# A gated linear attention with a MoE-style MLP behind it: every queue ordered by a list-scheduling model, loads reordered, dummy matmuls first, groups of 2 chunks

## The chip, the cores and the metric

One core of a Trainium2 chip. The metric is the device time of one execution in microseconds (us). A ratio is the mean time of one kernel's fast runs over that of the other's fast runs of the same rounds, so it is not quite the ratio of the medians that are quoted. A span is the profiled execution's time; it is mostly 1.6 to 2 us less than the time of the run. Rounds are the turns in which kernels were measured together.

## The reference

```python
# attention: batch 4, 8 heads, 768 steps, head_dim 48
for t in range(S):
    state = alpha[:, :, t, :, None] * state + einsum('bhd,bhe->bhde', k[:, :, t], v[:, :, t])
    y[:, :, t] = einsum('bhd,bhde->bhe', q[:, :, t], state)
# MLP on x = y as 3072 tokens x 384
h = x @ w_in            # w_in 384 x 2048
g = maximum(h, 0) ** 2
out = g @ w_out         # w_out 2048 x 384, float32 out
```

## The kernel before

The recurrence is done in 24 chunks of 128 steps. For chunk `s` the kernel takes the logarithm of alpha, sums it with a triangular matmul, and scales q and k by the exponentials ("decay"); transposes both ("transpose"); forms masked scores and updates the state ("scores"); multiplies scores by v ("intra"); and transposes the result `xn` into `xT_big` ("xT"). The MLP then makes first products (`ph`, three matmuls each, followed by a relu on ScalarE and a square on VectorE or GpSimd) and second products (`po`, 16 matmuls for 128 tokens, issued in quarters of 4). The MLP works on groups of 1, 2 and then 3 chunks. A bank is one of the PSUM buffers that matmuls write to. The code is cut ("...") and condensed.

```python
ps_misc: 2 banks   ps_sc: 1 buffer   ps_st: 1   ps_h: 2 banks (ph)   ps_o: 1 bank (po)

def load_chunk(sc):                       # four loads of 192 KB
    for nm, src in (("at", ar), ("qt", qr), ("kt", kr), ("vt", vr)):
        t = loads.tile([P, H, D], FP32, name=nm)           # bufs=4
        nc.sync.dma_start(out=t, in_=src[b, c])
def mm(*a, **kw):                         # only TensorE keeps the program's order;
    tc.keep_in_program_order(nc.tensor.matmul(*a, **kw))   # the framework orders the others
...
def st_decay(s):
    nc.scalar.activation(L[:, :, 0:D], at, AF.Ln)
    mm(pm[:, 0:HD], lhsT=utri_b[:, 0, :], rhs=L[:, :, 0:D], start=True, stop=True)
    ...
    nc.scalar.activation(A, pm3, AF.Exp)
    nc.scalar.activation(Ainv, pm3, AF.Exp, scale=-1.0)
    ...
    nc.vector.tensor_mul(qA_s[:, i, :, 0:D], qt, A)
    nc.vector.tensor_mul(kI_s[:, i, :, 0:D], kt, Ainv)
...
def moe1(g, f):                           # a first product
    for j in range(KT):
        mm(ph[:, 0:n], lhsT=w_in_b[:, j, f * P:(f + 1) * P], rhs=xT_big[:, j, t0:t0 + n], ...)
    nc.scalar.activation(r[:, 0:n], ph[:, 0:n], AF.Relu)
    eng = nc.vector if f % 2 == 0 else nc.gpsimd
    eng.tensor_mul(gT_tiles[g][:, f, 0:n], r[:, 0:n], r[:, 0:n])
...
GN = [1, 2, 3, 3, 3, 3, 3, 3, 3]          # chunks of each MLP group
...
for s in range(2):                        # order of the loads
    load_chunk(s)
    for pc in range(2 * s, 2 * s + 2):
        load_w_in(pc, 4)
load_chunk(2); load_w_out(0, 4); load_w_out(1, 4)
st_decay(0)
for s in range(NT):
    if s + 3 < NT: load_chunk(s + 3)
    if s < 2: load_w_out(s + 2, 4)
    seq = [st_transpose(s), st_scores(s), st_decay(s + 1), st_intra(s), st_xT(s)]   # as lambdas
    for k, f in enumerate(seq):
        f()
        moe_until(budget(s + (k + 1) / 5))      # MLP work spread evenly between the five stages
```

## Time and profile before

| | before |
|---|---|
| time, median of the first 3 runs | 225.64 us |
| span of the profiled run | 223.2 us |
| matmul work done by 40 / 80 / 190 us | 10.4 / 40.9 / 137.8 us |
| all matmul work | 165.4 us |

"Matmul work" is my count, used in the whole document: each matmul is given the time from its start to the next start when nothing holds it up. In the traces of before that is, as a median at full clock, 162 ns at 384 columns, 109 at 256, 56 at 128, and 42 or 43 at 96. The times that the count took are about half a nanosecond longer for the larger ones; with the medians themselves all the work comes to 165.2 us, where 165.4 are told, and the loss between 80 and 190 us to 13.3 us, where 13.1 are told. The matmuls of 48 columns and of 1 column take 25 ns each here (medians); the eight score matmuls take 330 ns together. Time in which this work does not advance, or advances at half clock, is "lost". (The expectations below use an earlier count that gave each score matmul 65 ns instead of 41. It showed about 2.5 us too little lost between 80 and 190 us for every kernel: 10.5 where the right count is 13.1, and 1.3 where it is 3.9. Counts of work are good to about 0.2 us, which is what a matmul that straddles the end of a stretch can shift.)

The page of before: span; busy time by engine; then the matmul engine's busy tenths, the granted clock, the DMA's busy tenths and its GB/s, in 40 slices of 5.6 us.

```profile
span 223.2 us, 4722 instructions
...
PE 184.1 (83%) x1744; PEld 117.6 (53%) x1744; DVE 129.9 (58%) x265; ACT 125.4 (56%) x325; POOL 70.9 (32%) x109
...
PE   1057659668998898999889989999989999999994
...
PEclk9999656999999999999999999999999999999999
DMA  6999999999895384989689853543100010010011
GB/s 134 294 216 269 224 264 244 262 190 208 184 220 123 73 185 99 180 180 215 145 174 206 177 110 85 133 106 62 47 35 3 37 38 35 0 40 35 37 71 71
```

Matmul busy time says 83%, but it counts more than work: a lone matmul of 384 columns is shown busy for 0.33 us, and in a stream one starts every 0.16 us. By work, 165 of 223 us are needed. The first 50 us are plainly thin. They are also where the DMA is busy, and where the granted clock is low: half from 24.3 to 37.9 us. The first clock record of this trace is at 20.9 us, and the 9s of the clock row before that stand for missing records. From 17.1 to 20.7 us, matmuls of 128 columns start 107 ns apart and not 56, so they ran at half rate there too. By my count 8.4 us of work were done at half rate by 40 us, which costs as much time again.

The timeline of before, from 3.7 to 12.5 us: start, duration, engine, line, operation, result<-operands, and the idle time before it with what ended it.

```profile
3.68 0.52 ACT L141 ACTIVATE L_s<-at 128x384 bf16<-128x384 f32 x1 [1.59 <-DMA at<-in_alpha_dram]
...
4.25 0.48 PE L128 MATMUL misc<-L_s,utri_b 128*128 128x384 bf16 x1 [4.25 <-ACT L_s L141]
...
4.85 0.49 ACT L152 ACTIVATE A<-misc 128x384 bf16<-128x384 f32 x1 [0.65 <-PE misc L128]
...
10.52 0.62 ACT L107 CAST w_in_b<-win_f 128x512 bf16<-128x512 f32 x1 [5.18 <-DMA win_f<-in_moe_w_in_dram]
...
11.04 0.48 ACT L154 ACTIVATE Ainv<-misc 128x384 bf16<-128x384 f32 x1
11.20 0.55 DVE L158 TENSOR_TENSOR qA_s<-qt,A 128x384 bf16<-128x384 f32 x1
...
11.89 0.58 PE L131 MATMUL misc<-ident_bf,qA_s 128*128 128x128 bf16 x4 [7.08 <-DVE qA_s L158]
```

ScalarE started `A` at 4.85 us. The next instruction in its queue was the cast of a w_in piece, which landed at 10.5 us. `Ainv`, whose input was long ready, stood behind it, and with it the tensor engine: 7.08 us. ScalarE did not pass the cast: it sat idle for 5.18 us before it, ran it at 10.52 us and took `Ainv` at 11.04.

Whom the matmuls waited for between 80 and 190 us in before: total us, times, longest.

```profile
PE ph L128 <- ACT r L243: 2.5, 11, 0.2
PE misc L131 <- ACT xn L220: 1.6, 3, 0.5
PE po L128 <- DVE ob L264: 1.5, 4, 0.4
...
```

And its weight loads, for the same stretch of before (a weight load that waits can hold the matmul behind it: one of `xn` starts at 115.99 us, after a wait of 0.90 us, and its matmul at 116.00):

```profile
...
PEld L131 <- ACT xn L220: 5.1, 9, 0.9
PEld L128 <- DVE qkT L171: 1.8, 4, 0.4
...
```

The line left out at the top puts 8.7 us more of the weight loads' idle time down to "issue", that is, to nothing that the profile shows. No single wait rules; the waits are many and short, 0.9 us at most, and 13.1 us are lost in 110. (The two lists overlap, so their sums are not to be added.)

### The profile page before, as it was taken

The numbers are of one execution on the slowest core, as the hardware profiler recorded it, in microseconds if no ns is written. First come the engines' busy times: TensorE is split into PE (matmuls) and PEld (weight loads), VectorE is DVE, ScalarE is ACT, GpSimd is POOL, SyncE is SP. The second block draws the span as 40 slices with busy tenths as digits, with TensorE's granted clock in tenths as the row PEclk, the third lists the DMA queues.
The fourth block names the chain that finished last, engine by engine and source line by source line (L and its number), as shares of the span: only waits on it lengthen the run. The fifth ranks groups of instructions, "written<-read, shape, count | busy, mean of one in ns | idle before, by whom it ended". The sixth has DMA issues, their size and how long they took to land.

```text
span 223.2 us, 4722 instructions
## 1 busy us (share of the span) xinstructions
PE 184.1 (83%) x1744; PEld 117.6 (53%) x1744; DVE 129.9 (58%) x265; ACT 125.4 (56%) x325; POOL 70.9 (32%) x109
## 2 busy tenths in 40 slices
PE   1057659668998898999889989999989999999994
PEld 0036537446654565555556555656655565555552
DVE  0188465777877675657576766557747665422300
ACT  4154666676657865764665576467456546544400
POOL 4012212233443333333431452334144222343310
PEclk9999656999999999999999999999999999999999
DMA  6999999999895384989689853543100010010011
GB/s 134 294 216 269 224 264 244 262 190 208 184 220 123 73 185 99 180 180 215 145 174 206 177 110 85 133 106 62 47 35 3 37 38 35 0 40 35 37 71 71
DMA packets 107031, 30.19 MB, mean 135 GB/s; under 512 B 100352, under 2 KB 105472, under 8 KB 107008
## 3 DMA queue, kind: packets, MB, share of 16 engines
q1 hardware_dynamic: 107008, 29.89, 57.8%
q8 instruction: 13, 0.21, 0.4%
q14 instruction: 10, 0.08, 0.1%
HBM read 25.17 MB, written 4.72 MB: 134 GB/s over the span
## 4 chain that ended last, share of the span: by engine, by line
PE 50%; ACT 27%; DVE 10%; issue 7%; DMA 3%; SPq 1%; ACTq 0%; DVEq 0%
PE po L128 19%; PE ph L128 14%; ACT r L243 8%; PE misc L128 6%; PE misc L131 6%; ACT A L152 4%; PE sc L128 4%; ACT Ainv L154 4%; ACT xn L220 3%; DVE qkT L171 3%; DMA win_f<-in_moe_w_in_dram 3%; DVE ob L264 3%; ACT L_s L141 2%; ACT sb L207 2%; PE st L128 2%
## 5 line engine op out<-in xcount | busy, mean ns | idle before, releaser
L243 ACT ACTIVATE r<-ph 128x384 bf16<-128x384 f32 (+2 forms) x144 | 64.3, 458 | 59.5 <-PE ph L128 55.6
L128 PE MATMUL ph<-xT_big,w_in_b 128*128 128x384 bf16 (+2 forms) x432 | 85.9, 318 | 6.2 <-ACT r L243 5.0
L128 PEld LDWEIGHTS <-w_in_b 128*128 128x128 bf16 x432 | 38.2, 102 | 23.3 <-issue 6.9
L187 DVE TENSOR_TENSOR sm<-sc,utri_b 128x512 bf16<-128x512 f32 x48 | 31.1, 685 | 5.5 <-PE sc L128 5.0
L143 POOL CAST vb<-vt 128x384 bf16<-128x384 f32 x24 | 15.0, 624 | 19.7 <-DMA vt<-in_v_dram 12.5
L152 ACT ACTIVATE A<-misc 128x384 bf16<-128x384 f32 x24 | 11.8, 490 | 14.0 <-PE misc L128 14.0
L171 DVE COPY qkT<-misc 128x1024 bf16<-128x1024 bf16 x24 | 16.5, 685 | 5.5 <-PE misc L131 5.2
L158 DVE TENSOR_TENSOR qA_s<-qt,A 128x384 bf16<-128x384 f32 x24 | 13.6, 568 | 9.3 <-ACT A L152 9.3
L128 PE MATMUL misc<-L_s,utri_b 128*128 128x384 bf16 x24 | 8.3, 346 | 11.3 <-ACT L_s L141 11.3
L128 PEld LDWEIGHTS <-qkT 64*128 64x128 bf16 (+1 forms) x272 | 9.9, 99 | 12.2 <-DVE qkT L171 6.4
L131 PE MATMUL misc<-ident_bf,qA_s 128*128 128x128 bf16 x96 | 10.2, 234 | 7.1 <-DVE qA_s L158 7.1
L159 DVE TENSOR_TENSOR kI_s<-kt,Ainv 128x384 bf16<-128x384 f32 x24 | 13.6, 567 | 2.1 <-ACT Ainv L154 2.1
L141 ACT ACTIVATE L_s<-at 128x384 bf16<-128x384 f32 x24 | 12.7, 527 | 1.7 <-DMA at<-in_alpha_dram 1.6
L264 DVE COPY ob<-po 128x384 f32<-128x384 f32 x16 | 8.8, 548 | 8.1 <-PE po L128 8.1
L131 PE MATMUL misc<-ident_bf,xn 128*128 128x128 bf16 x72 | 8.6, 232 | 5.7 <-ACT xn L220 5.5
L131 PEld LDWEIGHTS <-qA_s 128*128 128x128 bf16 x96 | 7.9, 106 | 9.5 <-issue 7.1
L128 PEld LDWEIGHTS <-L_s 128*128 128x128 bf16 x96 | 6.1, 99 | 12.5 <-issue 10.0
L228 DVE COPY xT_big<-misc 128x384 bf16<-128x384 bf16 x24 | 8.5, 355 | 7.2 <-PE misc L131 7.1
L128 PE MATMUL sc<-qkT 64*128 64x128 bf16 x192 | 10.2, 229 | 2.2 <-DVE qkT L171 1.5
L154 ACT ACTIVATE Ainv<-misc 128x384 bf16<-128x384 f32 x24 | 11.9, 496 | 0.0
L220 ACT CAST xn<-misc 128x384 bf16<-128x384 f32 x24 | 11.5, 478 | 0.4 <-PE misc L128 0.3
L245 POOL TENSOR_TENSOR gT_2836<-r 128x384 bf16<-128x384 bf16 x8 | 6.6, 827 | 15.9 <-ACT r L243 15.9
(71 smaller groups left out, 306.5 us busy)
## 6 DMA issues: line engine op xcount, KB each, us to landing
at<-in_alpha_dram SPq DMA_DIRECT2D x24, 192.0 KB, 3.9
qt<-in_q_dram SPq DMA_DIRECT2D x24, 192.0 KB, 3.6
kt<-in_k_dram SPq DMA_DIRECT2D x24, 192.0 KB, 3.8
vt<-in_v_dram SPq DMA_DIRECT2D x24, 192.0 KB, 3.9
out_dram<-ob SPq DMA_DIRECT2D x24, 192.0 KB, 1.9
win_f<-in_moe_w_in_dram SPq DMA_DIRECT2D x4, 768.0 KB, 7.3
wout_f<-in_moe_w_out_dram SPq DMA_DIRECT2D x4, 768.0 KB, 6.1
```

Source lines behind the costliest of these rows:

```text
L128: tc.keep_in_program_order(nc.tensor.matmul(*a, **kw))
L131: tc.keep_in_program_order(nc.tensor.transpose(*a))
L141: nc.scalar.activation(L[:, :, 0:D], at, AF.Ln)
L143: nc.gpsimd.tensor_copy(vb, vt)
L152: nc.scalar.activation(A, pm3, AF.Exp)
L154: nc.scalar.activation(Ainv, pm3, AF.Exp, scale=-1.0)
L158: nc.vector.tensor_mul(qA_s[:, i, :, 0:D], qt, A)
L171: nc.vector.tensor_copy(qkT, pT)
L187: nc.vector.tensor_mul(sm[:, hh], sc_ps[:, hh], utri_b.to_broadcast([P, NP, P]))
L220: nc.scalar.copy(xn, py[:, 0:HD])
L243: nc.scalar.activation(r[:, 0:n], ph[:, 0:n], AF.Relu)
L264: nc.vector.tensor_copy(ob, po)
```

## The change

The intent: the kernel holds a small model of the core (engine, duration, latency, bank and dependences of each operation), list-schedules all operations with it at build time (again and again it takes, of the operations left, the one that can start first), and emits every engine's instructions in that order, pinned. Loads of chunks 0 and 1 come before the weights, nine dummy matmuls run first, MLP groups have 2 chunks, and buffers are deeper. The diff is cut to its core and condensed; most of it rewrites the same operations as entries of the model.

```diff
+class Plan:
+    def run(self, gate):                 # of all engines, the operation that can start first
+        ...
+                    key = (max(r, t0), op.prio)
+        ...
+        self.order.sort(key=lambda o: o.start)
-    loads = ctx.enter_context(tc.tile_pool(name="loads", bufs=4))
-    wload = ... bufs=3        work ... bufs=2     rpool ... bufs=4    NBUF = 3
+    loads = ctx.enter_context(tc.tile_pool(name="loads", bufs=LB))       # LB = 6
+    wload = ... bufs=4        work ... bufs=4     rpool ... bufs=6    NBUF = 4
+    def pin(ins):
+        tc.keep_in_program_order(ins)    # for ScalarE, VectorE and GpSimd too
...
+        ln = d["use_at"] = add("ACT", 0.41, e_ln, d["ld_at"], old, prio=-5.0)
+        a_ = add("ACT", 0.39, e_A, p0, **g)              # g: prio=-10 + 0.01 s
+        mq = d["use_qt"] = add("DVE", 0.47, e_qA, a_, d["ld_qt"], old, **g)
+        rl = add("ACT", (72 + n) / 1200.0, e_relu, op, prio=-20.0)
...
-    GN = [1, 2, 3, 3, 3, 3, 3, 3, 3]
+    GN = [2, 2, 2, 2, 2, 2, 2, 2, 2, 2, 2, 2]
...
+        add("OUT", 0.55, e_out, ev)      # a store; on the same queue as the loads
+    DMA_ORDER = [0, 1, "i", "i", "i", "i", 2, 3, "o", "o", "o", "o"]   # then chunks 4, 5, ...
+    LEAD = 5                             # attention may be 5 chunks ahead of the MLP
+    def gate(op):
+        s = getattr(op, "gla", None)
+        if s is not None:
+            return s <= LEAD + (prog["m1"] + prog["m2"]) / 5.12
+        return True
...
+    wp = ps_o.tile([P, 512], FP32, name="po")
+    for _ in range(9):
+        mm(wp, lhsT=warm[:, 0:P], rhs=warm, start=True, stop=True)
+    for op in plan.order:
+        op.emit()
```

## The prediction

> **What bounds the kernel now.** The span is 223.2 us[...]. In the timeline three 384-column matmuls last 0.65 us together, one alone 0.33, so each takes 0.16 us of the array. [...] Counted so, the matmuls need about 165 us: 123 for the MoE products, 41 for attention. The other 58 us are idle or half-clock time:
>
> 1. Start: I count 16 us of useful matmul work by 50 us, 10 by 40. DMA is 0.8 to 1.0 busy there (busy by stretch): load waits, made worse by order. The scalar queue stands from 5.35 to 10.52 us behind a cast that waits for a w_in piece, though chunk 0 is in (timeline); the tensor queue waits 7.1 us behind it, and twice 2.6 us for alpha (23.6, 33.0 us). The granted clock is 0.5 from 24.3 to 37.9 us.
> 2. Middle, 60 to 200 us: 0.88 of full rate; short waits for relu output, xn, the qkT copy, the one output bank.
> 3. End: 3.3 us of eviction and store.
>
> **What the change does.** MoE work hardly changes: 192 relus of 256 columns (0.28 us each back to back, an estimate) replace 112 of 384 (0.38) and 32 smaller; some more ScalarE time, not critical. Nine dummy matmuls [...]move the first real one from 4.25 to about 5 us[...]. Worth about 0.
>
> Start: chunks 0, 1, then all w_in, chunks 2, 3, then all w_out. At the page's 220 to 290 GB/s, w_in is in by 20 us, chunks 2, 3 by 27, w_out by 38, chunk 5 by 46. Second products start at about 39 us, but by then four attention chunks and first products for four chunks, 17 us of work, can be done, against 10 now. At 65 us I expect 38 us of work done, against 28 now: 10 us gained.
>
> Middle: per chunk the tensor queue becomes transposes, state, 2 first products, a quarter of a second product, scores, 2, a quarter, decay, and so on. Between an attention step and its dependant lie 1.3 to 3 us of other matmuls; the chain to cover ([...]vector copy 0.69 or two masks 1.3 us) fits. First products come in pairs with a quarter (0.65 us) between, which covers the two-bank relu loop (about 1.0 us). I expect 0.945 of full rate, worth about 9 us. The kernel's model ignores [...]stores waiting in the load queue, so it won't be perfect.
>
> End: unchanged.
>
> Sum: 38.5 us of work at 65 us; 126 left at 0.945 = 133.5; end 3.4: span about 202, time 204 us. Range 197 to 213. Faster by over 2%: 0.95; within: 0.04; slower: 0.01.
>
> **What would show it.** Right: no 5 us hole on ScalarE before 11 us; chunk 1 finished by 16 us; matmul busy 9 in nearly all slices from 40 us on; tensor waits for relu and xn shrink; clock 1.0 from 38 us or before. Wrong: tensor holes at 45 to 65 us waiting for alpha or v loads stuck behind a store; waits for relu at each pair; a middle rate still near 0.88.
>
> **What would make it wrong.** Loads blocked by stores (213 or more); fixed queue orders that fit the chip badly, small waits adding up[...].

38.5 us of work at 65 us, 133.5 us for the rest and 3.4 us at the end made a span of about 202 us and a time of 204. What the traces show: in before, a relu that ScalarE waited for starts 0.26 us after the work of its product's last matmul is over (median of 70; for the work, see the count above). From the start of one relu to that of the next, back to back, 0.38 us pass at 384 columns (median of 15, before) and 0.28 at 256 (of 55, the changed kernel; in before 0.28 to whatever ScalarE did next, 10 times). The nine dummies of the changed kernel start 0.43 us apart, at 1.26 to 4.65 us.

## The result, and the profile after

| | before | changed |
|---|---|---|
| time, median | 225.41 us (4 runs) | 207.69 us (4 runs, 207.50 to 207.99) |
| ratio, 95% interval | | 0.9214 (0.9194 to 0.9234) |
| span | 223.2 us | 206.1 us |
| work done by 40 / 80 / 190 us | 10.4 / 40.9 / 137.8 us | 14.1 / 48.7 / 154.8 us |
| lost between 80 and 190 us | 13.1 us | 3.9 us |
| all matmul work, dummies not counted | 165.4 us | 165.8 us |

The page of the changed kernel, the same lines (slices of 5.2 us).

```profile
span 206.1 us, 5137 instructions
...
PE 185.6 (90%) x1897; PEld 133.9 (65%) x1897; DVE 140.0 (68%) x294; ACT 130.0 (63%) x377; POOL 76.2 (37%) x133
...
PE   7566964999979899999999999999999999999883
...
PEclk9855899699999999999999999999999999999999
DMA  7999999996799999999999996410111011100212
GB/s 129 189 356 317 170 281 379 196 197 125 153 213 199 197 216 189 213 178 220 166 225 184 202 216 130 110 38 0 41 38 45 0 41 38 41 16 23 76 41 76
```

Matmul busy time even rose, from 184.1 to 185.6 us, in a kernel that is 17 us shorter. So matmul busy time does not tell the loss here: the work is 165.4 and 165.8 us of spans of 223.2 and 206.1.

The slices also show two kinds of load. The weights come in rows of 2 KB or 1.5 KB and reach 317 to 379 GB/s (third, fourth and seventh slice); the chunks come in packets of 192 bytes (100,352 of the 107,032 packets are under 512 bytes), and the slices in which they are loaded stay at 166 to 225 GB/s at the same busy share (eighth, ninth and twelfth to 24th). The cause of the difference is not shown: no run changes the packets.

The timeline of the changed kernel over the same steps of chunk 0:

```profile
3.83 0.52 ACT L255 ACTIVATE L_s<-at 128x384 bf16<-128x384 f32 x1 [1.75 <-DMA at<-in_alpha_dram]
...
5.07 0.46 PE L180 MATMUL misc<-L_s,utri_b 128*128 128x384 bf16 x1
...
5.65 0.49 ACT L278 ACTIVATE A<-misc 128x384 bf16<-128x384 f32 x1 [1.30 <-PE misc L180]
6.04 0.48 ACT L282 ACTIVATE Ainv<-misc 128x384 bf16<-128x384 f32 x1
6.17 0.56 DVE L297 TENSOR_TENSOR qA_s<-qt,A 128x384 bf16<-128x384 f32 x1 [4.93 <-ACT A L278]
...
6.88 0.38 PE L183 MATMUL misc<-ident_bf,qA_s 128*128 128x128 bf16 x4 [1.26 <-DVE qA_s L297]
```

`Ainv` follows `A` at once; the first transposes start at 6.88 us and not at 11.89. The first real matmul is at 5.07, behind the dummies.

Whom the matmuls waited for between 80 and 190 us in the changed kernel:

```profile
PE ph L180 <- ACT r L416: 0.4, 2, 0.2
```

And its weight loads:

```profile
PEld L180 <- DVE qkT L314: 3.7, 10, 0.4
...
PEld L183 <- ACT xn L374: 0.4, 1, 0.4
```

The waits for `xn` and for the output bank are all but gone. The largest left is the one for the qkT copy, which grew (3.7 us on weight loads, 1.8 before). Its tensor queue for 3 of the 7 us of one chunk, from the timeline (MATMUL lines alone, so the weight loads and other engines between them are left out):

```profile
149.88 0.33 PE L180 MATMUL st<-vb,kI_s 128*128 128x96 bf16 x4
150.04 0.82 PE L180 MATMUL ph<-xT_big,w_in_b 128*128 128x256 bf16 x6
150.70 0.81 PE L180 MATMUL po<-w_out_b,gT_2513 128*128 128x384 bf16 x4
151.45 0.40 PE L180 MATMUL sc<-qkT 64*128 64x128 bf16 x8
151.78 0.83 PE L180 MATMUL ph<-xT_big,w_in_b 128*128 128x256 bf16 x6
152.44 0.81 PE L180 MATMUL po<-w_out_b,gT_2513 128*128 128x384 bf16 x4
153.09 0.33 PE L180 MATMUL misc<-L_s,utri_b 128*128 128x384 bf16 x1
```

Scores (`sc`) start 0.75 us after the last quarter did, and two first products (6 matmuls, 0.66 us to the next start) and a quarter lie between these attention steps (`st`, `sc`, and `misc<-L_s`, the decay).

One new wait shows at 59.5 us, again in the timeline:

```profile
59.52 0.52 ACT L255 ACTIVATE L_s<-at 128x384 bf16<-128x384 f32 x1 [1.59 <-DMA at<-in_alpha_dram]
59.95 0.64 ACT L416 ACTIVATE r<-ph 128x256 bf16<-128x256 f32 x2
...
60.37 0.49 PE L180 MATMUL ph<-xT_big,w_in_b 128*128 128x256 bf16 x3 [1.15 <-ACT r L416]
```

The logarithm of a later chunk stands in front of two relus and waits 1.59 us for its alpha; the tensor engine then waits 1.15 us for the relu.

Of the 17.1 us that the span lost, 3.7 were gained by 40 us (14.1 against 10.4 us of work), 4.1 more by 80 us, and 9.2 between 80 and 190 us; the end gives nothing. Of the 3.7 us by 40 us, 2.2 are less time at half clock: 6.2 us of work were done at half rate by then, against 8.4 before. The changed kernel had the full clock from 22.4 to 36.1 us, where the kernel before had half from 24.3 to 37.9. No run separates what the orders did there from how the clock happened to fall.

### The profile page after: what moved, and what is told of

It reads as the page before. It is cut to its first block, busy times and chain, and to the rows that moved or that the text cites. A ratio compares the mean times of both kernels' runs of the same rounds, so it can differ in the third digit from the quotient of the medians.

```text
span 206.1 us, 5137 instructions
## 1 busy us (share of the span) xinstructions
PE 185.6 (90%) x1897; PEld 133.9 (65%) x1897; DVE 140.0 (68%) x294; ACT 130.0 (63%) x377; POOL 76.2 (37%) x133
## 2 busy tenths in 40 slices
DMA packets 107032, 30.21 MB, mean 147 GB/s; under 512 B 100352, under 2 KB 105472, under 8 KB 107008
## 4 chain that ended last, share of the span: by engine, by line
PE 65%; DVE 9%; DMA 8%; ACT 6%; issue 5%; SPq 4%; POOL 2%; POOLq 0%; ACTq 0%; DVEq 0%
PE ph L180 26%; PE po L180 24%; PE misc L180 6%; PE misc L183 5%; DMA wst<-in_moe_w_in_dram 4%; SPq L241 3%; PE sc L180 3%; ACT r L416 3%; DMA at<-in_alpha_dram 2%; DVE qkT L314 2%; DMA vt<-in_v_dram 2%; DVE sm L330 2%; DVE ob L453 1%; DVE xT_big L385 1%; PE st L180 1%
## 5 line engine op out<-in xcount | busy, mean ns | idle before, releaser
L180 PE MATMUL ph<-xT_big,w_in_b 128*128 128x256 bf16 x576 | 84.7, 281 | 4.0 <-ACT r L416 2.8
L416 ACT ACTIVATE r<-ph 128x256 bf16<-128x256 f32 x192 | 68.5, 384 | 29.1 <-PE ph L180 27.6
L180 PEld LDWEIGHTS <-w_in_b 128*128 128x128 bf16 x576 | 53.0, 100 | 18.5 <-issue 6.5
L297 DVE TENSOR_TENSOR qA_s<-qt,A 128x384 bf16<-128x384 f32 x24 | 13.6, 570 | 10.8 <-ACT A L278 10.8
L300 DVE TENSOR_TENSOR kI_s<-kt,Ainv 128x384 bf16<-128x384 f32 x24 | 16.3, 683 | 1.7
L356 ACT CAST sb<-st 128x384 bf16<-128x384 f32 x20 | 9.5, 476 | 5.2 <-DVE st L351 5.2
L180 PE MATMUL misc<-vb,sm 128*128 128x48 bf16 x192 | 9.5, 186 | 3.5 <-DVE sm L330 3.5
L351 DVE TENSOR_TENSOR st<-st,ae_s 128x384 f32<-128x384 f32 x20 | 11.0, 552 | 0.0
L180 PEld LDWEIGHTS <-sm 128*128 128x128 bf16 x192 | 7.5, 98 | 4.6 <-DVE sm L330 4.3
L424 POOL TENSOR_TENSOR gT_592<-r 128x256 bf16<-128x256 bf16 x8 | 5.3, 657 | 13.7 <-ACT r L416 13.6
L183 PE MATMUL misc<-ident_bf,kI_s 128*128 128x128 bf16 x96 | 9.5, 223 | 0.8 <-DVE kI_s L300 0.7
```

The costliest lines, as they stand in the source:

```text
L180: pin(nc.tensor.matmul(*a, **kw))
L183: pin(nc.tensor.transpose(*a))
L297: pin(nc.vector.tensor_mul(qA[:, :, 0:D], d["qt"], d["A"]))
L300: pin(nc.vector.tensor_mul(kI[:, :, 0:D], d["kt"], d["Ai"]))
L416: pin(nc.scalar.activation(box["r"][:, 0:n], box["ph"][:, 0:n], AF.Relu))
```

## The experiments

Eleven edited kernels and one repeat (r_after), all correct. Changed kernel and before are the two bases. "Ratio" is always to the kernel before in the same rounds.

| run | base and edit | median us | ratio (95% interval) | work by 80 us | lost 80 to 190 us |
|---|---|---|---|---|---|
| before | | 225.4 to 226.0 by set of rounds | 1 | 40.9 | 13.1 |
| changed | | 207.69 | 0.9214 (0.9194 to 0.9234) | 48.7 | 3.9 |
| r_after | changed, again | 208.69 | 0.9244 (0.9210 to 0.9278) | 48.5 | 3.7 |
| e_nowarm | changed, no dummies | 208.17 | 0.9224 (0.9189 to 0.9259) | 47.7 | 3.6 |
| e_loads | changed, old load order | 211.51 | 0.9367 (0.9307 to 0.9426) | 43.8 | 3.8 |
| e_lateout | changed, stores later | 206.53 | 0.9146 (0.9103 to 0.9189) | 49.3 | 3.7 |
| e_unpin | changed, only TensorE pinned | 213.13 | 0.9426 (0.9374 to 0.9477) | 44.4 | 5.5 |
| e_gn3 | changed, old groups | 214.93 | 0.9526 (0.9448 to 0.9605) | 40.7 | 4.8 |
| e_lead2 | changed, lead 2 | 240.32 | 1.0665 (1.0607 to 1.0723) | 46.3 | 24.8 |
| e_relulast | changed, relu last | 209.22 | 0.9263 (0.9227 to 0.9299) | 46.9 | 2.8 |
| e_best4 | changed, stores later, lead 4 | 205.74 | 0.9116 (0.9082 to 0.9149) | 49.0 | 3.0 |
| b_gn2 | before, groups of 2 | 217.86 | 0.9665 (0.9612 to 0.9717) | 43.8 | 10.8 |
| b_loads | before, new loads | 224.43 | 0.9946 (0.9900 to 0.9992) | 41.2 | 13.1 |
| b_gl | before, both | 215.49 | 0.9557 (0.9519 to 0.9595) | 46.9 | 10.2 |

"Lost" is 110 us less the work done in that stretch. The work by 80 us also depends on the granted clock. The changed kernel runs at full clock from 39.5 us, but e_loads is at half clock from 37.0 to 47.2 us, e_unpin until 41.5 and from 68.8 to 72.2, and e_gn3 from 74.0 to 80.8. Between 40 and 80 us half clock makes up 3.2, 2.5 and 2.6 us of what they lose (the work that they did at half rate), and nothing of what the changed kernel loses. Whether the edits brought the half clock about is not shown.

### e_nowarm: the dummies

```diff
-    wp = ps_o.tile([P, 512], FP32, name="po")
-    for _ in range(9):
-        mm(wp, lhsT=warm[:, 0:P], rhs=warm, start=True, stop=True)
```

> The changed kernel without its nine dummy matmuls. My theory (the dummies are worth nothing, because the early phase waits for loads and the clock falls back after them): 207.7 us within 0.8 us, and the first real matmul starts near 4.3 us in place of 5.1. Rival (an early full clock shortens the first chunks): over 1.5 us slower, about 209.5 us or more.

Measured: 208.17 us, ratio 0.9224 against 0.9214 and 0.9244 for the changed kernel. The dummies are worth nothing that these runs can tell. The trace of the changed kernel fits my theory: its clock records grant full speed from 5.3 us for 3.4 us and half speed again from 8.8 to 22.4 us.

### e_loads and b_loads: the load order

```diff
-    DMA_ORDER = [0, 1, "i", "i", "i", "i", 2, 3, "o", "o", "o", "o"]
+    DMA_ORDER = [0, "i", "i", 1, "i", "i", 2, "o", "o", 3, "o", 4, "o"]    # e_loads
```
```diff
     for s in range(2):
         load_chunk(s)
-        for pc in range(2 * s, 2 * s + 2):
-            load_w_in(pc, 4)
-    load_chunk(2) ...
+    for pc in range(4):
+        load_w_in(pc, 4)
+    for s in range(2, 4):                # b_loads; 6 load buffers, 4 weight buffers,
+        load_chunk(s)                    # and in the loop, loads 4 chunks ahead, not 3
+    for pc in range(4):
+        load_w_out(pc, 4)
```

> The changed kernel with the load order of the kernel before (chunk 0, half of w_in, chunk 1, the rest of w_in, chunk 2, half of w_out, chunk 3 and so on); the kernel's model orders all queues around it. Theory 1 (the load order is what gained the 8 us by 80 us of time): about 212 to 215 us, with matmul work done by 80 us falling from 48.7 us to about 43. Theory 2 (the fixed queue orders, which no longer let a cast that waits for a load stand before ready work, gained them): within 2 us of 207.7.

> The kernel before with the load order of the changed one, its 6 load buffers and 4 weight staging buffers. Undoing the order in the changed kernel cost 3.8 us. Theory 1 (the load order acts by itself): 2 to 5 us faster than before, about 221 to 223.5, all of it by 80 us. Theory 2 (it only pays together with fixed queue orders): within 1 us of 225.5.

In the changed kernel the old load order costs about 3.8 us, just under the range of theory 1: work by 80 us falls by 4.9 us (the half clock after 40 us has 3.2 of them) and the middle stays as it was. In the kernel before, the new order gives 1.2 us (ratio 0.9946), between the two theories and hardly more than the differences that are not read here. In these two kernels, then, the order paid mostly where the rest of the queue could use it.

### e_unpin: are the other engines' orders needed?

```diff
     def pin(ins):
-        tc.keep_in_program_order(ins)
+        pass                             # mm() and tr() still pin TensorE
```

> The changed kernel with only the tensor queue kept in the order of the kernel's model; VectorE, ScalarE and GpSimd are left to the framework's scheduler, as in the kernel before. Theory 1 (the tensor queue's order, with enough other matmuls between a step and its dependant, is what gained the middle): within 2 us of 207.7. Theory 2 (the fixed orders of the other engines gained it): 3 us or more slower, with the tensor engine's waits for relu and xn back between 80 and 190 us.

By time theory 2 seems right (213.13 us), but not for its reason. Lost time in the middle rose by only 1.6 us, from 3.9 to 5.5; the rest of the loss, 4.3 us of work, came before 80 us, 2.5 of it as half clock. The waits for `xn` did not come back (none is listed; for relu 1.4 us against 0.4). The timeline of this run, with the framework's order of ScalarE:

```profile
3.84 0.52 ACT L255 ACTIVATE L_s<-at 128x384 bf16<-128x384 f32 x1 [1.76 <-DMA at<-in_alpha_dram]
...
8.32 0.52 ACT L255 ACTIVATE L_s<-at 128x384 bf16<-128x384 f32 x1 [3.96 <-DMA at<-in_alpha_dram]
8.75 0.47 ACT L278 ACTIVATE A<-misc 128x384 bf16<-128x384 f32 x1
...
9.96 0.59 PE L183 MATMUL misc<-ident_bf,qA_s 128*128 128x128 bf16 x4 [5.03 <-DVE qA_s L297]
```

The logarithm of chunk 1 (at 8.32) was put before `A` of chunk 0 (at 8.75). It waited 3.96 us for its alpha, and the tensor queue 5.03 us in turn. It is the fault of the kernel before with another culprit: an instruction that waits for a load in front of one that is ready.

### e_gn3 and b_gn2: the size of the groups

```diff
-    GN = [2, 2, 2, 2, 2, 2, 2, 2, 2, 2, 2, 2]
+    GN = [1, 2, 3, 3, 3, 3, 3, 3, 3]     # e_gn3; b_gn2 is the opposite edit on before
```

> The changed kernel with the MoE groups of the kernel before (1, 2, then 3 chunks each) in place of 2 chunks each; the model orders the queues around them. Theory 1 (the order of the tensor queue, not the group size, gained the middle): tensor time lost between 80 and 190 us stays under 4 us (it was 10.5 before, 1.3 after), total 208 to 211 us. Theory 2 (the 2-chunk groups gained it, since a group can start once two chunks are in): lost time back to 7 us or more, total 214 us or more.

> The kernel before with groups of 2 chunks and nothing else. Theory 1 (order): lost time between 80 and 190 us stays at 8 us or more, total within 2.5 us of 225.5. Theory 2 (groups): lost time falls to 4 us or less, total 219 us or less.

Here my theory, that only the order matters, fell by time in both kernels: old groups cost the changed kernel 7.2 us, and new groups gave the kernel before 7.7 us. It held for the middle: with old groups the changed kernel still loses only 4.8 us between 80 and 190 us (about 2.3 by the earlier count that the theory was stated in), and with new groups the kernel before still loses 10.8. What the groups of 2 give lies mostly before 80 us: in e_gn3 8.0 us of work are missing there, 7.0 of which (12.4 against 5.4 us lost) arise between 40 and 80 us, 2.6 of them as half clock from 74.0 us on. In b_gn2, 2.9 us are gained by 80 us, 2.3 in the middle and some at the end. One of the two longest waits of e_gn3 in that stretch, from its timeline:

```profile
75.15 0.48 PE L180 MATMUL st<-vb,kI_s 128*128 128x96 bf16 x4 [2.42 <-ACT sb L356]
```

The tensor queue has nothing but attention steps there, and one waits 2.42 us for the state copy of the chunk before. I read this as a 3-chunk group having no first products ready yet; the run shows the wait, not that reason.

### b_gl: groups and loads together, without the model

The two edits on before together (b_loads with groups of 2).

> The kernel before with the groups of 2 chunks and the load order and buffers of the changed one, still without fixed queue orders from the model. Alone the groups gave 7.7 us and the loads 1.2. Theory 1 (what is left, about 8 us, is the model's queue orders): 215.5 to 217.5 us, lost tensor time between 80 and 190 us stays near 8 us. Theory 2 (groups and loads together release more than their sum): 213 us or less.

215.49 us, at the edge of theory 1's range and slightly more than the sum of the parts (10.0 against 8.9 us). By 80 us it has done 46.9 us of work, nearly the changed kernel's 48.5 in the same rounds. What is left, 6.8 us of time against r_after, is the middle: 10.2 against 3.7 us lost. That is the share of the model's queue orders together with the deeper working buffers (`work` 4 for 2, `rpool` 6 for 4, NBUF 4 for 3), which b_gl lacks and which no run tested alone. Orders matter with those buffers held fixed: e_unpin loses 5.4 us of time and e_lead2 32.6. Whether the buffers have a part is not shown. Where b_gn2 still loses in the middle, its timeline shows (one case of 15, 8.35 us in all between 80 and 190 us):

```profile
133.29 0.81 PE L128 MATMUL ph<-xT_big,w_in_b 128*128 128x256 bf16 x6
133.46 0.49 ACT L152 ACTIVATE A<-misc 128x384 bf16<-128x384 f32 x1 [0.51 <-PE misc L128]
...
133.85 0.47 ACT L207 CAST sb<-st 128x384 bf16<-128x384 f32 x1
...
134.21 0.51 ACT L154 ACTIVATE Ainv<-misc 128x384 bf16<-128x384 f32 x1
...
134.96 0.66 ACT L243 ACTIVATE r<-ph 128x256 bf16<-128x256 f32 x2
...
135.40 0.82 PE L128 MATMUL ph<-xT_big,w_in_b 128*128 128x256 bf16 x6 [0.45 <-ACT r L243]
```

Two first products end at about 134.1 us, but their relus stand behind two exponentials, a state copy and two small exponentials (the last two left out here) that came first in ScalarE's order. The relus start at 134.96 us, and the next two first products need the same two banks. In the changed kernel's middle such a wait for relu is listed twice, 0.4 us in all, against 5.4 us in b_gl.

### e_lead2: the same model, another order

```diff
-    LEAD = 5
+    LEAD = 2
```

> The changed kernel with the one number in its model that says how many chunks the attention may run ahead of the MoE work cut from 5 to 2. The tensor queue then has runs of 7 and more first products followed by 6 quarters of second products, in place of pairs with a quarter between. Theory 1 (the middle is fast because pairs with a quarter between cover the two-bank relu loop of about 1 us): waits for relu come back, 0.15 to 0.2 us at each product inside a run, lost time between 80 and 190 us 6 to 10 us, total 212 to 218 us. Theory 2 (any complete order from the model does it): within 2 us of 207.7.

240.32 us: theory 1's direction, and worse than its range; slower than before by 6.7%. With one number changed the model emits runs of first products and then runs of second products. The tensor engine's timeline inside such a run:

```profile
131.78 0.82 PE L180 MATMUL ph<-xT_big,w_in_b 128*128 128x256 bf16 x6 [0.45 <-DVE xT_big L385]
132.79 0.82 PE L180 MATMUL ph<-xT_big,w_in_b 128*128 128x256 bf16 x6 [0.20 <-ACT r L416]
133.81 0.82 PE L180 MATMUL ph<-xT_big,w_in_b 128*128 128x256 bf16 x6 [0.20 <-ACT r L416]
```

Pairs of first products (6 matmuls) start every 1.01 to 1.02 us, where the changed kernel's pairs, with a quarter behind them, take 0.66: about 0.18 us lost at each product, as expected. The 24.8 us lost between 80 and 190 us hold more than that: waits between first products in such runs make up 13.7 us, and waits at attention steps most of the rest (3.7 us before a group's first product, which waits for `xT_big`, and 2.8 between transposes). So a complete order by a model is no gain in itself; this order was.

### e_relulast: a different priority

```diff
-        rl = add("ACT", (72 + n) / 1200.0, e_relu, op, prio=-20.0)
+        rl = add("ACT", (72 + n) / 1200.0, e_relu, op, prio=1.0)
```

> The changed kernel with the relu last instead of first in the model's choice among ready ScalarE work; the model re-orders the tensor queue to suit. Theory 1 (relu first is what keeps the first products from waiting on their two banks): lost time between 80 and 190 us rises from 1.3 to 4 us or more, total 210 us or more. Theory 2 (the model makes up for it by spacing the products): within 2 us of 207.7.

209.22 us, theory 2: in the same rounds the changed kernel took 208.69. The model moved the tensor queue's steps so that the relus still came in time (2.8 us lost in the middle). The priority of the relu is not what matters.

### e_lateout, r_after and e_best4: what the changed kernel still loses

```diff
-        self.order.sort(key=lambda o: o.start)
+        self.order.sort(key=lambda o: o.start + (10.0 if o.eng == "OUT" else 0.0))   # e_lateout
-    LEAD = 5
+    LEAD = 4                                                                         # e_best4, with both edits
```

> The changed kernel with each store emitted 10 us later in the order of the load queue, so that loads do not stand behind a store whose data is not ready. Theory 1 (the stretch from 48 to 70 us is slow because the load queue stood 3.1 us and more behind stores): 204.5 to 206 us, and the ScalarE's waits for alpha between 40 and 75 us fall from 4.4 us to under 2. Theory 2 (that stretch is bound by how fast the DMA delivers chunks): within 0.7 us of 207.7, the waits stay.

> The changed kernel once more, on the same chip as the next run, for a comparison under 1 per cent: 207.7 us within 0.7 us.

> The changed kernel with the stores emitted 10 us later (this alone measured 206.5 us) and the attention allowed to run 4 chunks ahead instead of 5, which spreads the attention steps between 45 and 75 us more evenly over the MoE work. Theory 1 (the loss left between 45 and 75 us is attention steps crowding on one another): 204 to 206 us. Theory 2 (it is the chunks' arrival): 206 to 207 us, as with the later stores alone.

Whom the load queue (SP) waited for between 40 and 80 us in the changed kernel, longest first:

```profile
SPq L460 <- DVE ob L453: 3.1, 1, 3.1
```

ScalarE's waits for alpha between 40 and 75 us in the changed kernel:

```profile
ACT L_s L255 <- DMA at<-in_alpha_dram: 4.4, 4, 1.6
```

The same of e_lateout:

```profile
ACT L_s L255 <- DMA at<-in_alpha_dram: 0.3, 1, 0.3
```

A store (L460) whose data was not ready held the loads behind it for 3.1 us; with the stores later, waits for alpha fall from 4.4 to 0.3 us. The time fell by less than expected: 206.53 us, ratio 0.9146. With the lead of 4 as well, 205.74 us against 208.69 for the changed kernel in the same rounds: ratios 0.9116 (0.9082 to 0.9149) and 0.9244 (0.9210 to 0.9278), which do not overlap. This version beats both kernels. Against e_lateout it is not told apart (the intervals overlap, and the rounds were others), so which theory of e_best4 holds stays open. Its waits for alpha between 40 and 75 us are 2.7 us, more than the 0.3 of e_lateout. r_after itself came out at 208.69 us, 1 us above its first measurement on another chip and outside the 0.7 us that I gave it; differences under about 1 us between runs of different rounds are not read here.

## Why the prediction was right, and where its terms were off

- **Size and direction.** 204 us was predicted (197 to 213), 207.69 measured. Two gains were named, start and middle; the trace shows both, of 7.8 us by 80 us and 9.2 us between 80 and 190 us. That the sum came out so near is in part luck: a gain that was not named, the groups of 2, is needed for it. With the old groups the same kernel takes 214.93 us (e_gn3), which is outside the range.
- **Start, "10 us gained" at 65 us.** At 65 us the work done is 35.2 against 28.4 us: 6.8 us gained, not 10. I expected 38.5. This term is the one that was mis-sized. The whole of it was missing by 39 us: 13.6 us of work and not 17. From 39 to 65 us the kernel did 21.6 us, as the sum has it (38.5 less 17). The loads were not far off: the last w_in cast ended at 22.3 us (w_in was expected in by 20), and second products started at 41.3 (39 predicted). But the work could not be packed as I summed it: chunk 1 was through only at 17.95 us (predicted 16), 6.2 us of work by 40 us ran at half clock, and from 27.8 to 36.0 us the tensor queue had only attention steps of chunks 2 and 3, with pauses of 0.3 to 0.9 us between them, 4.2 us in all. Alpha waits of up to 1.59 us came later, between 54 and 69 us. Stores held up the loads there, as the prediction named for the bad case, but a run with the stores moved recovers only 1 to 2 us (206.53 against 208.17 us for e_nowarm in the same rounds).
- **What gained the start.** I put it to the load order and to the end of ScalarE's wait behind a cast. The runs show a third: the groups of 2, which the prediction did not name as a gain (its "first products for four chunks" by 39 us needs them). Without them the changed kernel does no more work by 80 us (40.7) than before (40.9), though 2.6 us of that run's loss are half clock. The single effects do not add: old loads cost 3.8 us, unpinned engines 5.4, old groups 7.2 on a start gain of 7.8.
- **Middle, "0.945 of full rate", 9 us.** From 65 to 190 us the rate is 0.957 (119.6 us of work in 125); in before it is 0.875. The mechanism holds: waits for relu, `xn` and the output bank all but went, and b_gl, which has the groups and loads but neither the model's orders nor its working buffers, keeps 10.2 us of loss there. But in b_gl the output bank's wait is already gone and the waits for `xn` are down (0.5 us on matmuls and 1.0 on weight loads, against 1.6 and 5.1 before). What is left there is above all the wait for relu: 5.4 us on matmuls, against 2.5 before and 0.4 in the changed kernel. The pairs with a quarter between are supported by e_lead2, where runs without the quarter bring back 0.18 us at each product.
- **Dummies, "worth about 0".** Right: e_nowarm is within noise, the first real matmul of the changed kernel moved to 5.07 us, and the clock fell back at 8.8 us.
- **Signs to look for.** No 5 us hole on ScalarE before 11 us: right. Busy 9 in nearly all slices from 40 us: nearly, one shows 7 (57 to 62 us) and one 8 (67 to 72 us), besides the end. Clock at 1.0 from 38 us: from 39.5, and also between 22.4 and 36.1.
- **End, 3.4 us.** Eviction and store take 3.3 us as before.

## What to carry to other kernels

Look in the timeline for an instruction that waits for a load or a far engine in front of one that is ready; both slow starts and one late stall here were of this kind (ScalarE waited 5.18 us in before, 3.96 in e_unpin and 1.59 in the changed kernel). Choose an order of the tensor queue by the length of the loop that it must cover (bank, relu, bank again: 1.01 to 1.02 us for two banks in e_lead2) and put other matmuls of that length between; a model can find it, but its result must be measured, as one number in it turned an 8% gain into a 7% loss. A group size that looks like a detail of the arithmetic also decides when work becomes available.
